# Attention with two MLPs on one core: column sums placed behind the weight conversions, and a second product that follows four steps behind the first

## The chip, the cores and the metric

One core of a Trainium2 chip. A time is the device time of one execution in microseconds (us), the median of several runs. "PE" is TensorE, "DVE" VectorE, "ACT" ScalarE, "POOL" GpSimd and "SP" SyncE, which issues the DMAs. L99 is line 99 of the kernel before.

## The reference

Batch 4, 8 heads, 576 tokens of head dimension 64, so 2304 rows of 512 for the two MLPs (512 to 2048 to 512). All of it is float32.

```python
rel = pos[:, None] - pos[None, :]
mask = (rel >= 0) & (rel < 128)
scores = np.where(mask, q @ k.T / sqrt(64) + slopes * -np.abs(rel), -1e9)
attn = softmax(scores)            # by rows
x = (attn @ v), heads side by side # 2304 x 512

r = np.maximum(x @ w_in1, 0.0)
x = (s * (r * r) + b) @ w_out1     # first MLP: s and b are scalars
h = np.maximum(x @ w_in2, 0.0)
out = (h * h) @ w_out2             # second MLP
```

## The kernel before, in words

A float32 number is kept as two parts, a rounded `hi` and the rest `lo` (`split`, L96 to L102: ACT copies, DVE subtracts), and a product is three matmuls: hi by hi, lo by hi, hi by lo. The weights arrive as 64-bit words and are converted in the kernel by `convert` (L106 to L124): ACT L119, DVE L120, ACT L121, DVE L122, one POOL addition L123, then the split (ACT L99, DVE L102 into `wil` or `wol`). A weight matrix pair is four groups of four steps (`w..0` to `w..3`).

Tokens go through the first MLP in blocks of 256: `a0` to `a7`, and `a8`, which holds the four tails of 64 tokens. The blocks `a0` to `a2` are done in two halves (`a` for steps 0 to 7, `c` for 8 to 15), because the weights of the second half are not there yet. The attention of later blocks runs as pieces between the MLP's steps (matmuls at L245, L270 and L281; the softmax's DVE instructions at L186 to L194; L268 scales probabilities before PE transposes them at L270).

The function `mlp` (L334) makes one step out of `first` (12 matmuls into a PSUM tile `h`, L357; then ACT takes the relu at L367, DVE squares at L368, and the split writes a tile `g`) and one `last` (the 12 matmuls of the second product, L394 or L403, which read `g`). A list `todo` holds the steps whose second product is outstanding. A step's `last` follows when the list is longer than `LAG = 2` (one for wide steps of 512 tokens, L384). So between a step's first product and its second stand two other steps. Tiles `g` come from a tag with three buffers. Pieces of other work come in through the list `behind`, spread over a share `span` of the steps.

Since b is a scalar, its part in the first MLP's output is b times the column sums of `w_out1`. POOL forms them in `csum`: `sum_rows` (L499) adds the hi and the lo part of each of the 16 steps, 32 additions (L502). `sum_column` (L541) adds over the partitions with four matmuls by `ones` (`pc`, L544), and DVE makes `bcol`, which ACT adds at L531 when the first MLP's result is fetched for the second (`fetch`).

After the attention its pools are closed and a pool `bp` opens, with tiles `gw` of 512 tokens (two buffers). In that stage the blocks `a7` and `a8` run as two jobs side by side, `a8` six steps behind, while the second MLP's weights are fetched and converted through three buffers `st`. Then come the second MLP's blocks `b0`, `b1`, `b2` (512 tokens), `btail` (256) and `b3`.

Every instruction is recorded in program order, and a scheduler with a model of time then sets the order on each engine. `tc.issue_after(x)` makes it place what follows behind instruction x. An engine runs its instructions in that order, so a wait holds up all that stands behind it.

Of the kernel before, what the change touches and what calls it, by code (L numbers as in the profile page):

```python
# [8 lines left out]
F32 = mybir.dt.float32  # L9
F32R = mybir.dt.float32r  # L10
# [3 lines left out]
ALU = mybir.AluOpType  # L14
PSUM = bass.MemoryType.PSUM
P = 128
# [3 lines left out]
def attention_mlp2_kernel(ctx, tc, first0, first1, qkv0, qkv1, qkvt, w_in1, w_out1, s_in, b_in, w_in2, w_out2, out):  # L20
# [7 lines left out]
    nc = tc.nc  # L28
# [9 lines left out]
    BLK = 256  # L38
# [9 lines left out]
    mp = ctx.enter_context(tc.tile_pool(name="mp", bufs=2))  # L48
# [18 lines left out]
    csum = const.tile([P, DM], F32, tag="csum", name="csum")  # L67
# [23 lines left out]
    def split(hi, lo, src, copy, sub):  # L91
        copy(hi, src)
        sub(lo, src, hi.bitcast(F32))
# [10 lines left out]

    n_g = [0]

    marks = []

    def convert(words, hi, lo):

        l32, h32 = words[..., 0], words[..., 1]
        with tc.issue_after(marks[-4]) if len(marks) > 3 else nullcontext():
            nc.scalar.activation(l32, l32.bitcast(U32), AF.Copy, scale=2.0 ** -29)  # L119
        nc.vector.scalar_tensor_tensor(l32, h32, -2 ** 31, l32, ALU.bitwise_and, ALU.bitwise_or)  # L120
        nc.scalar.activation(h32.bitcast(F32), h32.bitcast(F32), AF.Copy, scale=2.0 ** -112)  # L121
        nc.vector.tensor_scalar(h32, h32, 3, None, ALU.logical_shift_left)  # L122
        nc.gpsimd.tensor_tensor(l32, h32, l32, ALU.add)  # L123
        split(hi, lo, l32.bitcast(F32), act_copy, dve_sub)  # L124

    last_load = []
# [3 lines left out]
    def group_loads(g, wts, w_in, w_out, staging, steps):  # L130
# [22 lines left out]
        def conv(i):  # L153
            _, k, n, step = parts[i]
            if k not in wts[g]:
                for j in (k, k + 1):
                    wts[g][j] = wp.tile([P, GF, DM], F32R, tag=f"{GTAGS[j]}{g}", name=f"{GTAGS[j]}{g}")
            hi, lo = wts[g][k], wts[g][k + 1]
            part = (slice(None), slice(n, n + step)) if k else (slice(None), slice(None), slice(n * P, (n + step) * P))
            convert(places.pop(i).rearrange("p a (n w) -> p a n w", w=2), hi[part], lo[part])  # L160
# [172 lines left out]
    def mlp(jobs, wts, second, fs, behind=(), span=0.8, lead=0, n_out=2):  # L333

        pos = [[psum("o", f"o{nm}{i}") for i in range(n_out)] for nm, _, _ in jobs]  # L340
        w = n_out * P if second is second_n else BLK
        behind = list(behind)
        todo, done, left, made = [], 0, len(behind), {}
        n_steps = max(1, int(len(fs) * len(jobs) * span))

        def first(f, n):
            nm, x, _ = jobs[n]
            if n not in made:
                made[n] = x() if callable(x) else x
            xh, xl = made[n]  # L350
            g, j = divmod(f, GF)
            wih, wil = wts[g][0], wts[g][1]
            ph = psum("h", f"h{nm}_{f}")[:, :w]
            k = 0
            for cc in range(NCC):
                for w_, x_ in ((wih, xh), (wih, xl), (wil, xh)):
                    nc.tensor.matmul(ph, w_[:, cc, j * P:(j + 1) * P], x_[:, cc, :],  # L357
                                     start=(k == 0), stop=(k == 3 * NCC - 1))
                    k += 1
            n_g[0] += 1  # L360
            if w > BLK:
                gh = pools["bp"].tile([P, 2, w], F32R, tag="gw", name=f"g{nm}_{f}")
                r = pools["bp"].tile([P, w], F32, tag="rw", name=f"r{nm}_{f}", bufs=1)
            else:
                gh = mp.tile([P, 2, BLK], F32R, tag="g", name=f"g{nm}_{f}", bufs=3)
                r = mp.tile([P, BLK], F32, tag="r", name=f"r{nm}_{f}")
            nc.scalar.activation(r, ph, AF.Relu)  # L367
            nc.vector.scalar_tensor_tensor(r, ph, 0.0, r, ALU.max, ALU.mult)  # L368
            split(gh[:, 0, :], gh[:, 1, :], r, act_copy, dve_sub)
            todo.append((f, n, gh))  # L370

        def last():
            f, n, gh = todo.pop(0)
            second(pos[n], wts[f // GF], f % GF, gh, f == fs[0], f == fs[-1])
            if f == fs[-1]:
                jobs[n][2](pos[n])

        order = sorted((k + lead * n, n, f) for n in range(len(jobs)) for k, f in enumerate(fs))
        for _, n, f in order:
            while len(behind) > left * max(0, n_steps - done - 1) // n_steps:  # L380
                behind.pop(0)()
            first(f, n)
            done += 1
            if len(todo) > (1 if w > BLK else LAG):  # L384
                last()
        while todo:
            last()
# [23 lines left out]
    def finish1(nm, dram):  # L411
        def f(po):
            for t in range(2):
                xo = result(f"xo{nm}{t}")
                act_copy(xo, po[t])
                nc.sync.dma_start(dram[:, 2 * t:2 * t + 2, :].rearrange("p a n -> p (a n)"), xo)
        return f
# [17 lines left out]
    LAG = 2  # L435
    FS = list(range(NF))
    wts1, wts2 = [], []
    pools = {"ps": ps}

    def psum(tag, name):  # L440
        return pools["ps"].tile([P, DM], F32, tag=tag, name=name)
# [18 lines left out]
    def half(i, behind, span=1):  # L460
        mlp([(f"a{i}", xs[i], finish1(f"a{i}", half_dram[i]))], wts1, second_t, FS[:HF], behind, span)

    def other(i, behind, span=1):
        mlp([(f"c{i}", xs[i], finish1(f"c{i}", acc_dram[i]))], wts1, second_t, FS[HF:], behind, span)
# [33 lines left out]
    nc.sync.dma_start(b_sb, b_in.partition_broadcast(P))  # L498
    def sum_rows(g, j):  # L499

        for w in (wts1[g][2], wts1[g][3]):
            nc.gpsimd.tensor_tensor(csum, csum, w[:, j, :].bitcast(F32), ALU.add)  # L502

    nc.gpsimd.memset(csum, 0.0)
    sums = [lambda g=g, j=j: sum_rows(g, j) for g in range(NG) for j in range(GF)]
    tails = [[lambda b=b, hp=hp: tail_unit(b, hp) for hp in range(H // 2)] for b in range(B)]
    for i in range(NHALF, LAST - 1):
        more = attn(i + 2) if i + 2 < LAST and i + 2 > 4 else []
        pending += tails[i - 3] if i > 2 else []
        mlp([(f"a{i}", xt.pop(blocks[i]), finish1(f"a{i}", acc_dram[i]))], wts1, second_t, FS, zipped((pending + more[:5], 2), (sums[:4], 1)))  # L510
        pending = more[5:]
        del sums[:4]
# [4 lines left out]
    bp = pools["bp"] = ctx.enter_context(tc.tile_pool(name="bp", bufs=2))  # L517
    n_g[0] = -1

    def fetch(nm, drams, scaled=True):  # L520

        xi = bp.tile([P, NCC, BLK], F32, tag="xi", name=f"xi{nm}")
        with tc.issue_after(last_load[0]) if last_load else nullcontext():
            nc.sync.dma_start(xi, drams[0])
        if len(drams) > 1:
            for o in range(0, NCC, 2):
                xj = bp.tile([P, 2, BLK], F32, tag="xj", name=f"xj{nm}{o}", bufs=1)
                nc.sync.dma_start(xj, drams[1][:, o:o + 2, :])
                nc.vector.tensor_tensor(xi[:, o:o + 2, :], xi[:, o:o + 2, :], xj, ALU.add)
        for o in range(NCC if scaled else 0):  # L530
            nc.scalar.activation(xi[:, o, :], xi[:, o, :], AF.Identity, bias=bcol[:, o:o + 1], scale=s_sb)  # L531
        return xi
# [14 lines left out]
    def fetch_y(i):  # L547
        return fetch(f"b{i}", [acc_dram[i]] + half_dram[i:i + 1])

    def load_y(b):  # L550
# [5 lines left out]
    y0 = []  # L556
    mlp([(f"a{i}", xt.pop(blocks[i]), finish1(f"a{i}", acc_dram[i])),
         (f"a{LAST}", x_tail, finish1(f"a{LAST}", acc_dram[LAST]))], wts1, second_t, FS,
        [sum_column] + [lambda u=u: y0.append(fetch_y(u)) for u in range(2)], 0.9, 6)

    def in_bp(i, nm):
        return bp.tile([P, 1, 2 * DM], I32, tag="st", name=nm, bufs=3)
# [62 lines left out]
```

## Time and profile before

| | us |
|---|---|
| median of 3 runs (1007.28, 1007.93, 1010.74) | 1007.93 |
| the profiled execution | 1010.16 |
| its span, first to last instruction | 1008.4 |
| PE busy in it | 974.3 |
| DVE, ACT, POOL busy | 522.2, 490.2, 130.4 |

Busy time of PE is modelled with the length of a matmul in the pipeline, so a busy PE can still start its matmuls later than it could. How many matmuls start in a stretch, beside the distance of two of them where nothing waits, tells more. A row of a timeline gives the start, the length, the engine, the line and the tiles, and in brackets the idle time ahead of it and what ended that.

### The profile page before, as it was taken

The numbers are of one execution on the slowest core, as the hardware profiler recorded it, in microseconds if no ns is written. First come the engines' busy times: TensorE is split into PE (matmuls) and PEld (weight loads), VectorE is DVE, ScalarE is ACT, GpSimd is POOL, SyncE is SP. The second block draws the span as 40 slices with busy tenths as digits, with TensorE's granted clock in tenths as the row PEclk, the third lists the DMA queues.
The fourth block names the chain that finished last, engine by engine and source line by source line (L and its number), as shares of the span: only waits on it lengthen the run. The fifth ranks groups of instructions, "written<-read, shape, count | busy, mean of one in ns | idle before, by whom it ended". The sixth has DMA issues, their size and how long they took to land.

```text
span 1008.4 us, 16815 instructions
## 1 busy us (share of the span) xinstructions
PE 974.3 (97%) x6504; PEld 854.1 (85%) x6504; DVE 522.2 (52%) x1236; ACT 490.2 (49%) x1157; POOL 130.4 (13%) x118
## 2 busy tenths in 40 slices
PE   6899889999999999999999899999999999999997
PEld 4689778999989999899999888778888888898886
DVE  6997998443564444544265787754223222432222
ACT  7977766454555445554355666664222312322221
POOL 4653655000000000000010312310000000000000
PEclk9799989999999999999999999999999999999999
DMA  8135423111221211211052444422000100100001
GB/s 333 43 129 167 162 88 106 53 53 35 60 67 46 72 34 52 75 54 39 9 184 74 131 173 147 147 83 74 11 1 5 59 1 0 43 1 22 1 1 42
DMA packets 46928, 72.39 MB, mean 72 GB/s; under 512 B 6656, under 2 KB 27136, under 8 KB 46848
## 3 DMA queue, kind: packets, MB, share of 16 engines
q1 hardware_dynamic: 46848, 71.32, 21.8%
q8 instruction: 51, 0.84, 0.3%
q14 instruction: 29, 0.24, 0.1%
HBM read 59.77 MB, written 11.53 MB: 71 GB/s over the span
## 4 chain that ended last, share of the span: by engine, by line
PE 75%; DVE 9%; DMA 9%; ACT 4%; issue 2%; SPq 0%; POOL 0%; ACTq 0%; DVEq 0%; POOLq 0%
PE ob L403 15%; PE hb L357 14%; PE ha L357 13%; PE oa L394 13%; DMA st<-w_in 4%; PE oc L394 3%; PE s L245 3%; PE hc L357 3%; PE u L281 3%; DMA st<-w_out 2%; PE hbtail L357 2%; PE t L270 2%; PE obtail L403 2%; DVE wol L102 1%; DVE wil L102 1%
## 5 line engine op out<-in xcount | busy, mean ns | idle before, releaser
L394 PE MATMUL oa<-ga,woh 128*128 128x256 f32 x960 | 189.6, 289 | 7.3 <-ACT ga L99 3.9
L403 PE MATMUL ob<-woh,gb 128*128 128x512 f32 x512 | 168.9, 391 | 1.4 <-ACT gb L99 1.3
L394 PEld LDWEIGHTS oa<-ga,woh 128*128 128x128 f32 x960 | 152.2, 192 | 14.0 <-DVE ga L102 5.2
L394 PE MATMUL oa<-ga,wol 128*128 128x256 f32 x480 | 135.6, 286 | 0.1
L368 DVE SCALAR_TENSOR_TENSOR rb<-hb,rb 128x512 f32<-128x512 f32 x64 | 44.1, 690 | 147.4 <-ACT rb L367 147.2
L403 PEld LDWEIGHTS ob<-woh,gb 128*128 128x128 f32 x512 | 95.9, 188 | 23.8 <-ACT gb L99 3.3
L367 ACT ACTIVATE rb<-hb 128x512 f32<-128x512 f32 x64 | 38.2, 597 | 156.5 <-PE hb L357 152.0
L123 POOL TENSOR_TENSOR st<-st 128x512 int32<-128x512 int32 (+1 forms) x50 | 70.3, 1407 | 235.1 <-DVE st L122 177.4
L403 PE MATMUL ob<-wol,gb 128*128 128x512 f32 x256 | 99.7, 389 | 0.0
L394 PEld LDWEIGHTS oa<-ga,wol 128*128 128x128 f32 x480 | 92.2, 192 | 1.2 <-issue 0.9
L368 DVE SCALAR_TENSOR_TENSOR ra<-ha,ra 128x256 f32<-128x256 f32 x120 | 50.0, 419 | 62.9 <-ACT ra L367 62.4
L102 DVE TENSOR_TENSOR ga<-ra,ga 128x256 fp32r<-128x256 f32 x120 | 65.8, 552 | 29.0 <-ACT ga L99 28.4
L99 ACT ACTIVATE ga<-ra 128x256 fp32r<-128x256 f32 x120 | 49.5, 416 | 42.4 <-DVE ra L368 41.7
L102 DVE TENSOR_TENSOR gb<-rb,gb 128x512 fp32r<-128x512 f32 x64 | 45.5, 711 | 44.0 <-ACT gb L99 43.8
L367 ACT ACTIVATE ra<-ha 128x256 f32<-128x256 f32 x120 | 45.0, 378 | 43.6 <-PE ha L357 39.0
L99 ACT ACTIVATE gb<-rb 128x512 fp32r<-128x512 f32 x64 | 40.4, 632 | 47.7 <-DVE rb L368 35.6
L120 DVE SCALAR_TENSOR_TENSOR st<-st 128x512 int32<-128x512 int32 (+1 forms) x50 | 47.3, 950 | 26.3 <-ACT st L119 25.8
L119 ACT ACTIVATE st<-st 128x512 int32<-128x512 uint32 (+1 forms) x50 | 40.5, 814 | 35.2 <-DMA st<-w_out 19.3
L403 PEld LDWEIGHTS ob<-wol,gb 128*128 128x128 f32 x256 | 48.1, 188 | 9.7
L190 ACT ACTIVATE pr<-pr,nd 128x256 f32<-128x256 f32 (+1 forms) x96 | 45.1, 473 | 3.8 <-DVE nd L186 3.4
L121 ACT ACTIVATE st<-st 128x512 f32<-128x512 f32 (+1 forms) x50 | 40.5, 813 | 7.0 <-DVE st L120 7.0
L186 DVE CUSTOM_DVE_ANT_0 pr<-s,bases 128x256 f32<-128x256 f32 (+1 forms) x96 | 32.1, 386 | 19.4 <-PE t L270 15.0
(204 smaller groups left out, 2387.1 us busy)
## 6 DMA issues: line engine op xcount, KB each, us to landing
st<-w_out SPq DMA_DIRECT2D x20, 512.0 KB, 3.9
st<-w_in SPq DMA_DIRECT2D x8, 1024.0 KB, 6.8
st<-w_in SPq DMA_DIRECT2D x16, 512.0 KB, 4.8
st<-w_out SPq DMA_DIRECT2D x6, 1024.0 KB, 8.9
raw<-qkv SPq DMA_DIRECT2D x36, 128.0 KB, 2.6
xib<-acc SPq DMA_DIRECT2D x9, 512.0 KB, 4.4
out<-obb SPq DMA_DIRECT2D x16, 256.0 KB, 2.0
raw<-qkv SPq DMA_DIRECT2D x24, 160.0 KB, 2.9
```

The source lines that it names most:

```text
L99: return nc.scalar.activation(o, i, AF.Copy)
L102: nc.vector.tensor_tensor(o, a, b_, ALU.subtract)
L119: nc.scalar.activation(l32, l32.bitcast(U32), AF.Copy, scale=2.0 ** -29)
L120: nc.vector.scalar_tensor_tensor(l32, h32, -2 ** 31, l32, ALU.bitwise_and, ALU.bitwise_or)
L121: nc.scalar.activation(h32.bitcast(F32), h32.bitcast(F32), AF.Copy, scale=2.0 ** -112)
L123: nc.gpsimd.tensor_tensor(l32, h32, l32, ALU.add)
L190: nc.scalar.activation(pr, pr, AF.Exp, bias=nmx, scale=-1.0, accum_out=den)
L357: nc.tensor.matmul(ph, w_[:, cc, j * P:(j + 1) * P], x_[:, cc, :], start=(k == 0), stop=(k == 3 * NCC - 1))
L367: nc.scalar.activation(r, ph, AF.Relu)
L368: nc.vector.scalar_tensor_tensor(r, ph, 0.0, r, ALU.max, ALU.mult)
L394: nc.tensor.matmul(po[o // 2][:, (o % 2) * BLK:(o % 2 + 1) * BLK], w_[:, j, o * P:(o + 1) * P], g[:, gi, :], start=(start and n == 0 and o ...
L403: nc.tensor.matmul(po[t], g[:, gi, t * P:(t + 1) * P], w_[:, j, :], start=(start and n == 0), stop=(stop and n == 2))
```

## The change

It does four things.

- `sum_rows` is placed behind the last POOL addition of the first MLP's conversions (`issue_after(adds[-1])`). It is the same 32 additions.
- Once `bp` is open, steps of 256 tokens lag by four instead of two. That is the stage of `a7` and `a8`, and `btail`.
- For that, five tiles `g` live at once: of every five steps in that time, two take a tile of tag `gw` and use half of it.
- In the list of `a7` and `a8`, two empty pieces come first and the span is 0.6 instead of 0.9, so `sum_column` comes at step 7 instead of step 0, and the two fetches at steps 11 and 15 instead of 9 and 18.

```diff
@@ def convert
-        nc.gpsimd.tensor_tensor(l32, h32, l32, ALU.add)
+        adds.append(nc.gpsimd.tensor_tensor(l32, h32, l32, ALU.add).ins)
@@ def mlp, first
-                gh = mp.tile([P, 2, BLK], F32R, tag="g", name=f"g{nm}_{f}", bufs=3)
+                if "bp" in pools and n_g[0] % 5 > 2:
+                    gh = pools["bp"].tile([P, 2, 2 * BLK], F32R, tag="gw", name=f"g{nm}_{f}")[:, :, :BLK]
+                else:
+                    gh = mp.tile([P, 2, BLK], F32R, tag="g", name=f"g{nm}_{f}", bufs=3)
@@ def mlp
-            if len(todo) > (1 if w > BLK else LAG):
+            if len(todo) > (1 if w > BLK else 4 if "bp" in pools else LAG):
@@ def sum_rows
-        for w in (wts1[g][2], wts1[g][3]):
-            nc.gpsimd.tensor_tensor(csum, csum, w[:, j, :].bitcast(F32), ALU.add)
+        with tc.issue_after(adds[-1]):
+            for w in (wts1[g][2], wts1[g][3]):
+                nc.gpsimd.tensor_tensor(csum, csum, w[:, j, :].bitcast(F32), ALU.add)
@@ the call of mlp for a7 and a8
-        [sum_column] + [lambda u=u: y0.append(fetch_y(u)) for u in range(2)], 0.9, 6)
+        [lambda: None] * 2 + [sum_column] + [lambda u=u: y0.append(fetch_y(u)) for u in range(2)], 0.6, 6)
```

The order on the engines, at three places. First POOL, before: a piece of its queue while the weights of group 2 are converted (`st..` are staged weights at L123, `csum` the sums).

```order
L123 TENSOR_TENSOR st21_1102<-st21_1102 128x1024
L123 TENSOR_TENSOR st22_1225<-st22_1225 128x1024
L502 TENSOR_TENSOR csum_90<-csum_90,woh2_1475 128x512
L123 TENSOR_TENSOR st23_1258<-st23_1258 128x1024
L502 TENSOR_TENSOR csum_90<-csum_90,wol2_1476 128x512
```

And POOL in the change, at the end of the first MLP's conversions (L124 is the old L123, L507 the old L502).

```order
L124 TENSOR_TENSOR st31_1676<-st31_1676 128x1024
L124 TENSOR_TENSOR st33_1751<-st33_1751 128x512
L124 TENSOR_TENSOR st34_1815<-st34_1815 128x512
L124 TENSOR_TENSOR st35_1817<-st35_1817 128x512
L507 TENSOR_TENSOR csum_90<-csum_90,woh0_317 128x512
L507 TENSOR_TENSOR csum_90<-csum_90,wol0_318 128x512
```

All 32 additions to `csum`, which stood between the 14 conversions from `st10` to `st35`, now follow `st35` one after another.

Second DVE, before: the queue around the first squares of block `a0` (`ra0_0`, `ra0_1`), which free the PSUM tiles that PE's next step writes.

```order
L120 SCALAR_TENSOR_TENSOR st11_480<-st11_480 128x1024
L193 TENSOR_SCALAR nd0_1_2_553<-nd0_1_2_553 128x4
L194 RECIPROCAL nd0_1_2_553<-nd0_1_2_553 128x4
L368 SCALAR_TENSOR_TENSOR ra0_0_362<-ha0_0_348,ra0_0_362 128x256
L268 TENSOR_SCALAR f0_1_2woh_554<-f0_1_2woh_554,nd0_1_2_553 128x256 x2
L102 TENSOR_TENSOR wil1_340<-st10_337,wih1_339 128x4x256
L368 SCALAR_TENSOR_TENSOR ra0_1_429<-ha0_1_415,ra0_1_429 128x256
```

And the same place in the change.

```order
L121 SCALAR_TENSOR_TENSOR st11_480<-st11_480 128x1024
L194 TENSOR_SCALAR nd0_1_2_553<-nd0_1_2_553 128x4
L195 RECIPROCAL nd0_1_2_553<-nd0_1_2_553 128x4
L269 TENSOR_SCALAR f0_1_2woh_554<-f0_1_2woh_554,nd0_1_2_553 128x256 x2
L102 TENSOR_TENSOR wil1_340<-st10_337,wih1_339 128x4x256
L372 SCALAR_TENSOR_TENSOR ra0_0_362<-ha0_0_348,ra0_0_362 128x256
L372 SCALAR_TENSOR_TENSOR ra0_1_429<-ha0_1_415,ra0_1_429 128x256
```

The first square now stands behind the two scalings (old L268) and behind a weight subtraction. Such exchanges are found on PE, ACT and DVE up to the first steps of `c0` and `c1`; from there to the end of `a6` the order is the same.

Third PE, before: the second product of step 5 of block `a8` (`ga8_5`) in the stage with two jobs.

```order
L357 MATMUL ha8_6_6827<-xtailh_6224,wih1_339 128x256
L357 MATMUL ha8_6_6827<-xtaill_6225,wih1_339 128x256
L357 MATMUL ha8_6_6827<-xtailh_6224,wil1_340 128x256
L394 MATMUL oa80_6230<-ga8_5_6766,woh1_709 128x256 x2
L394 MATMUL oa80_6230<-ga8_5_6766,wol1_710 128x256
```

And the same second product in the change.

```order
L358 MATMUL ha8_7_6865<-xtailh_6224,wih1_339 128x256
L358 MATMUL ha8_7_6865<-xtaill_6225,wih1_339 128x256
L358 MATMUL ha8_7_6865<-xtailh_6224,wil1_340 128x256
L398 MATMUL oa80_6230<-ga8_5_6754,woh1_709 128x256 x2
L398 MATMUL oa80_6230<-ga8_5_6754,wol1_710 128x256
```

It followed the first product of `a8`'s step 6, and now follows that of step 7.

## Rows read from the trace of the kernel before

**Rows 1.** The page, part 1: busy us, share of the span and instructions of each engine.

```profile
PE 974.3 (97%) x6504; PEld 854.1 (85%) x6504; DVE 522.2 (52%) x1236; ACT 490.2 (49%) x1157; POOL 130.4 (13%) x118
```

**Rows 2.** Timeline of PE, 491 to 498 us (start, length): two matmuls, no waits.

```profile
495.12 0.28 PE L357 MATMUL ha<-x3h,wil 128*128 128x256 f32 x1
495.24 0.28 PE L357 MATMUL ha<-x3h,wih 128*128 128x256 f32 x1
```

**Rows 3.** Busy time by stretch; the first row names the columns.

```profile
core 0: us, PE busy (x) PEld busy (x) DVE busy (x) ACT busy (x) POOL busy (x), PEclk, DMA share, GB/s
40.00:60.00 20.00, 16.33 (x122) 13.37 (x121) 19.79 (x27) 14.72 (x32) 16.50 (x9) 0.91 0.47 174
120.00:140.00 20.00, 14.94 (x101) 12.09 (x100) 19.15 (x29) 13.07 (x28) 14.07 (x10) 0.83 0.55 177
165.00:211.00 46.00, 45.94 (x397) 42.61 (x396) 24.54 (x75) 23.41 (x65) 3.20 (x3) 1.00 0.20 59
560.00:600.00 40.00, 34.59 (x259) 32.04 (x258) 30.21 (x53) 26.80 (x58) 8.55 (x8) 1.00 0.46 152
```

**Rows 4.** Timeline of PE, 125 to 134 us: the first and last of three stalls.

```profile
130.13 0.41 PE L270 MATMUL t<-ident,pr 128*128 128x128 f32 x2 [1.65 <-DVE pr L268]
...
132.82 1.11 PE L270 MATMUL t<-ident,pr 128*128 128x128 f32 x4 [0.75 <-ACT pt L99]
```

**Rows 5.** Timeline of DVE, 120 to 136 us: the chain ahead of those stalls.

```profile
125.30 2.05 DVE L102 TENSOR_TENSOR wol<-st,woh 128x1024 fp32r<-128x1024 f32 x1 [0.17 <-ACT woh L99]
127.27 0.41 DVE L102 TENSOR_TENSOR x1l<-u,x1h 128x256 fp32r<-128x256 f32 x1
127.60 0.92 DVE L193 TENSOR_SCALAR nd<-nd 128x4 f32<-128x4 f32 x1
...
128.77 4.17 DVE L268 TENSOR_SCALAR pr<-pr,nd 128x256 f32<-128x256 f32 x4
```

**Rows 6.** Timeline of DVE, 160 to 176 us: kinds of instruction of rows 5, undisturbed.

```profile
168.56 1.13 DVE L268 TENSOR_SCALAR pr<-pr,nd 128x256 f32<-128x256 f32 x4
...
175.28 0.17 DVE L193 TENSOR_SCALAR nd<-nd 128x4 f32<-128x4 f32 x1 [0.38 <-ACT pr L190]
```

**Rows 7.** Timeline of DVE, 40 to 54 us.

```profile
40.09 1.22 DVE L102 TENSOR_TENSOR wol<-st,woh 128x1024 fp32r<-128x1024 f32 x1
...
44.50 2.48 DVE L120 SCALAR_TENSOR_TENSOR st<-st 128x1024 int32<-128x1024 int32 x1
46.90 1.23 DVE L193 TENSOR_SCALAR nd<-nd 128x4 f32<-128x4 f32 x1
...
48.57 2.42 DVE L268 TENSOR_SCALAR f_2woh<-f_2woh,nd 128x256 f32<-128x256 f32 x2
```

**Rows 8.** Groups of instructions by line, POOL: the column sums.

```profile
L502 POOL TENSOR_TENSOR csum<-csum,woh 128x512 f32<-128x512 f32 x16 | 25.2, 1573 | 8.4 <-ACT woh L99 7.8
L502 POOL TENSOR_TENSOR csum<-csum,wol 128x512 f32<-128x512 f32 x16 | 23.4, 1460 | 4.9 <-DVE wol L102 4.1
```

**Rows 9.** Groups by line and form, DVE, 165 to 215 us: one instruction per attention piece.

```profile
L193 DVE TENSOR_SCALAR nd<-nd 128x4 f32<-128x4 f32 x4 | 1.8, 442 | 1.4 <-ACT pr L190 1.4
```

**Rows 10.** Timelines of DVE and PE, 190 to 214 us: scaling, then transposes.

```profile
196.57 1.13 DVE L268 TENSOR_SCALAR pr<-pr,nd 128x256 f32<-128x256 f32 x4
...
200.04 0.38 PE L270 MATMUL t<-ident,pr 128*128 128x128 f32 x2
```

**Rows 11.** Timeline of PE, 555 to 606 us: two of its six stalls.

```profile
562.08 0.50 PE L394 MATMUL oa<-ga,woh 128*128 128x256 f32 x2 [0.93 <-ACT ga L99]
...
576.02 0.50 PE L394 MATMUL oa<-ga,woh 128*128 128x256 f32 x2 [1.54 <-ACT ga L99]
```

**Rows 12.** Timeline of ACT, 555 to 600 us, ahead of the first of them.

```profile
561.05 0.68 ACT L119 ACTIVATE st<-st 128x512 int32<-128x512 uint32 x1 [0.95 <-DMA st<-w_out]
561.63 0.40 ACT L99 ACTIVATE ga<-ra 128x256 fp32r<-128x256 f32 x1
```

**Rows 13.** Timeline of PE, 498 to 606 us: the sum column.

```profile
503.70 1.05 PE L544 MATMUL pc<-ones,csum 128*128 128x1 f32 x8 [0.75 <-ACT xoa L99]
```

More of the change, by code (lines that the diff above doesn't have):

```diff
@@ L105, in attention_mlp2_kernel @@
     n_g = [0]
+    adds = []
     marks = []
```

## The prediction

> **What bounds the kernel now.** I read the page's busy times first, then the granted clock and PE's busy share by stretches, then PE's stalls one by one, and last what the engine that PE waited for was doing. PE is the bound: it is busy for 974.3 of 1008.4 us, DVE for half the span and POOL for an eighth [rows 1]. So a change can gain only where PE waits, where its clock is down, or where its matmuls start later than they could. Where nothing waits, two matmuls of 256 columns start 0.12 us apart [rows 2]; a step of 24 takes 2.88 us. Three stretches stand out [rows 3]. From 40 to 60 us PE is idle for 3.67 us, and the granted clock averages 0.91. From 120 to 140 us it is idle for 5.06 us with the clock at 0.83: a third of that time, 6.8 us, at 1.2 GHz instead of 2.4, which is 3.4 us of work. In both DVE is busy for over 19 of 20 us and POOL for 14 to 16. From 560 to 600 us PE starts 259 matmuls, worth 31.1 us at 0.12, with a clock of 1.00; a few are wide ones, so some 8 us are lost there, 5.41 of them as idle time. From 165 to 211 us PE is idle for 0.06 us, with a clock of 1.00.
>
> **The column sums.** What holds PE up at 130 us is read from DVE. PE's transposes wait for the scaling at L268 [rows 4]. Four scalings take 4.17 us there [rows 5] and 1.13 us where no addition of POOL runs beside them [rows 6]; the small instruction at L193 takes 0.92 against 0.17; the weight subtraction takes 2.05 against 1.22 [rows 7]. That is 3.04 + 0.75 + 0.83 = 4.6 us on one chain without a gap, while POOL adds column sums back to back. An instruction that reads PSUM at the same time (`x1l`) takes its usual 0.41 us [rows 5]. So it is the sums, 25.2 + 23.4 = 48.6 us on POOL [rows 8], that hold DVE's SBUF work, and the order shows that all 32 leave this stretch. Of the 4.6 us I take 3.8, since the last stall of the three ends with ACT and not with DVE [rows 4]; of the 3.4 us of clock I take 2.7, since PE idles before the sums too. Sum: **6.5 us gained** at 120 to 140 us. Bounds: 2 (only the first stall of 1.65 us goes, and something else is late next) and 8 (all of the chain and of the clock).
>
> From 40 to 60 us the same three kinds of instruction are long: 2.48 at L120, 1.23 at L193, 2.42 for two scalings [rows 7], some 4.1 us above their usual lengths (1.2 as the subtraction of the same size, 0.17 and 0.6). But in the new order the square that frees PE's PSUM tile stands behind the two scalings (0.6) and a weight subtraction (1.2), where it stood ahead of them; and conversions, which stay, hold DVE as the sums do. I take **0**, with bounds of 4.1 gained and 1.8 lost. The exchanges of order up to 100 us, where DVE is as full, I count into these bounds.
>
> **Where the sums go.** They run in one block after the last conversion, at about 161 us, and their 48.6 us reach to about 210 or later. The stretch from 165 to 211 us has DVE busy for 24.5 of 46 us and PE without idle time [rows 3], so there is room, but the attention goes on: four pieces with one L193 each [rows 9] and four scalings. By rows 5 and 6 a piece's chain grows by up to 0.75 + 3.04 = 3.8 us. In the undisturbed trace the scalings end at 197.70 and the transposes start at 200.04 [rows 10], 2.3 us later. What is left is 1.5 us of stall a piece; for the three pieces that lie well inside the block, **4.5 us lost**. Bounds: 0 (the room takes it all) and 18.6 (four pieces at 3.8, and one fall of the clock as at 131 us, 3.4). I take the value nearer to the lower end because the slack is seen in a row, and DVE is half free.
>
> Here a rule of the notes speaks against the change. The Trainium skill, page "SBUF — State Buffer", section "Who interferes with whom", says that VectorE and GpSimd share one pair of ports, that the one that starts first keeps it for its whole instruction, and that the other is blocked. The trace agrees on which instructions are held: the scaling is, the one with a PSUM input is not. By the rule alone the same 32 additions hold the port as long after the move as before it; the sum would then be the next term by itself, 6 us gained, and the case is the second rival.
>
> **Lag of four.** The six stalls from 560 to 600 us are of one kind: a second product waits for `g` from ACT or DVE, 0.39 to 1.54 us [rows 11]. ACT copied that `g` late, since it had stood on a conversion whose DMA was late by 0.95 us [rows 12]. These are waits for something late, not for something slow: ACT works 26.8 and DVE 30.2 of the 40 us [rows 3]. Two more steps of distance are 2 x 2.88 = 5.76 us, more than any of the stalls. But if the stretch shrinks from 40 to 32 us, the same 30.2 us of DVE would fill it to 94 per cent, so not all comes back. **6 us gained**; bounds 2 and 8. The price of the lag, second products that free the weights' tiles and PSUM later, lies inside the stage: a tile of weights comes free two steps later on that account, and the stage's waits, which now fall away, are as long. In `btail` PE has no wait to lose, and the borrowed tiles are idle then: 0.
>
> **The sum column** costs the same matmuls at step 7 as at step 0. Its wait of 0.75 us [rows 13] ended with ACT's copy out of PSUM, for a tile that the next product `ha7_0` now writes first; the wait passes to that product. 0, with a bound of 0.75 gained.
>
> **Sum.** -6.5 + 0 + 4.5 - 6 + 0 = -8.0 us. The profiled execution took 1010.16 us, of which the span is 1008.4; it would take 1002.2. It lies 2.2 us above the median of the runs shown, 1007.93, so against the median the forecast is **999.9 us, say 1000**.
>
> **The rivals.**
>
> The block stalls PE (slower). All four pieces behind 161 us pay the full 3.8 us, and the clock falls once: 18.6 us instead of 4.5. For it: the same chain at 125 to 133 us cost about that much, for one piece. Against it: DVE is half free, and slack is seen. The sum is then +6.1, 1014 us. It decides against the change from 12.5 us of cost on, beyond which the two gains are spent, and shows as slower from 15.5. Chance 0.09.
>
> The move is worth nothing. The sums hold DVE as long in the block as they did before, and PE waits there for the 6.5 us that it gains at 130 us: each of the four pieces costs 1.6 us instead of the 1.5 of three. The sum is then the lag's -6, and the time 1001.9 us. For it: the additions are the same 32, and their 48.6 us are longer than the 46 in which PE has no wait. Against it: DVE is busy for over 19 of 20 us where they stand now, and for half the time where they will. Chance 0.12.
>
> The lag only shifts the wait. ACT and DVE work at their rate, not late, and what PE wins before 600 us it waits for in `b0`, whose steps lag by one as before. Then the lag gives 2, and the sum is -4: 1004 us. For it: the 94 per cent. Against it: the conversions are not bound to this stretch. Chance 0.20.
>
> The block hides. DVE's free half takes it, and both gains come whole: -8 - 8 = -16, 992 us. For it: PE idles nowhere from 165 to 211 us. Against it: transposes follow scalings by 2.3 us only. Chance 0.20.
>
> The change does not do what it says: new stalls of the exchanged order before 100 us take back what the sums give, and the lag gives the 2 us: about 1007. Chance 0.06.
>
> **How the numbers follow.** My forecast has the other 0.33. Its own range, with the bounds of its terms, is 994 to 1006. For 8 in 10 the range reaches to the hiding block and to the shifted wait, and leaves out the slower rival and the lowest end: **990 to 1009**. About 0.3 per cent, 3.0 us, can be told from no change, so faster means under 1004.9. The forecast lies there nearly whole (0.31), the worthless move mostly (0.11), of the shifted wait two thirds (0.13), and the hiding block (0.20): 0.75. Slower is the first rival with a little of the rest, 0.10. The same is what remains, 0.15.
>
> **What would show it.** Right: from 120 to 140 us no addition at the old L502, four scalings in about 1.2 us, PE idle under 2 us and a clock near 1.00; from 161 us on 32 additions in a row, scalings of up to 4 us, and a few PE waits on L268; from 560 to 600 us no PE wait over 0.3 us and the stage some 6 us shorter; `ha7_0` ahead of `pc` with the wait of about 0.7 us. Wrong: PE idle for over 8 us between 160 and 220 us, or a loss in `b0` as large as the gain before it, or stalls between 60 and 100 us, where there are none now.

## The result, and the profile after

| | before | change |
|---|---|---|
| median, us | 1009.18 (7 runs, 1007.28 to 1010.74) | 1015.3 (7 runs, 1012.57 to 1020.97) |
| the profiled execution, us | 1010.16 | 1018.52 |
| its span, us | 1008.4 | 1016.7 |

The change is slower: the ratio is 1.0065, with a 95% interval of 1.0041 to 1.0090. The forecast was 1000 us with a range of 990 to 1009.

PE does the same work; the same engine is the bound as in [rows 1]. The page, part 1, of the changed kernel:

```profile
PE 978.9 (96%) x6504; PEld 858.5 (84%) x6504; DVE 526.6 (52%) x1236; ACT 489.5 (48%) x1157; POOL 125.4 (12%) x118
```

Busy time by stretch in the changed kernel (columns as in [rows 3]), with one more stretch, that of `b0`:

```profile
core 0: us, PE busy (x) PEld busy (x) DVE busy (x) ACT busy (x) POOL busy (x), PEclk, DMA share, GB/s
40.00:60.00 20.00, 19.70 (x143) 16.55 (x143) 15.91 (x31) 16.00 (x34) 3.98 (x3) 0.81 0.46 174
120.00:140.00 20.00, 16.15 (x105) 13.66 (x104) 14.91 (x30) 15.30 (x31) 3.10 (x2) 0.74 0.51 166
165.00:211.00 46.00, 39.45 (x309) 36.72 (x310) 36.61 (x61) 18.00 (x49) 39.40 (x29) 0.93 0.15 44
560.00:600.00 40.00, 39.98 (x332) 39.66 (x331) 31.01 (x55) 28.94 (x61) 9.82 (x9) 1.00 0.52 173
600.00:680.00 80.00, 72.59 (x326) 56.94 (x326) 59.30 (x88) 51.69 (x92) 18.98 (x19) 1.00 0.40 128
```

And that stretch in the kernel before:

```profile
600.00:680.00 80.00, 78.64 (x367) 64.11 (x366) 55.05 (x88) 53.17 (x94) 20.17 (x18) 1.00 0.40 125
```

Against [rows 3]: at 40 to 60 us PE is idle for 0.30 us instead of 3.67, but the clock is 0.81 instead of 0.91. At 120 to 140 us it is idle for 3.85 instead of 5.06, with a clock of 0.74 instead of 0.83. From 165 to 211 us it is idle for 6.55 instead of 0.06, and the clock has fallen to 0.93: this is the block. From 560 to 600 us it is idle for 0.02 instead of 5.41. From 600 to 680 us it is idle for 7.41 instead of 1.36.

Idle time leaves out a slow clock, so I also use the **loss**: for each matmul of a trace, how much later the next one starts than is usual (the median) after a matmul of that shape in that trace, summed over a stretch. It counts waits and slow clock alike. In us:

| loss, us | 0-40 | 40-160 | 160-200 | 200-560 | 560-600 | 600-680 | all |
|---|---|---|---|---|---|---|---|
| before | 21.9 | 19.9 | 2.0 | 10.9 | 8.4 | 3.1 | 66.0 |
| change | 22.0 | 17.6 | 11.5 | 12.0 | 1.0 | 10.6 | 74.7 |

So the 8.3 us between the spans are +9.6 at the block, -2.3 ahead of it, -7.4 from 560 to 600 us, +7.5 in `b0`, and 1 us of small change between.

**The block.** Timeline of the changed kernel, 163 to 188 us, POOL, DVE and PE:

```profile
163.64 1.24 DVE L194 TENSOR_SCALAR nd<-nd 128x4 f32<-128x4 f32 x1
...
166.42 5.44 DVE L269 TENSOR_SCALAR pr<-pr,nd 128x256 f32<-128x256 f32 x4
...
167.74 1.28 POOL L507 TENSOR_TENSOR csum<-csum,wol 128x512 f32<-128x512 f32 x1
...
169.09 1.27 POOL L507 TENSOR_TENSOR csum<-csum,woh 128x512 f32<-128x512 f32 x1
...
172.64 0.85 PE L246 MATMUL s<-qk 64*128 64x256 f32 x10 [2.75 <-DVE qk L102]
...
181.47 5.30 DVE L269 TENSOR_SCALAR pr<-pr,nd 128x256 f32<-128x256 f32 x4
...
187.15 0.39 PE L358 MATMUL hc<-x0h,wih 128*128 128x256 f32 x1 [2.45 <-DVE rc L372]
```

Four scalings (old L268) take 5.44 and 5.30 us, against 1.13 undisturbed [rows 6] and 4.17 in the kernel before [rows 5]: each waits for about one whole addition of 1.27 or 1.28 us. But PE's longest waits, 2.75 and 2.45 us, end with the split of `qk` and with a square, DVE instructions that stand behind the scalings in its queue. That a DVE instruction which runs in a mode with two ports, as `tensor_scalar` can, or which has two inputs in SBUF, is held for a whole POOL instruction is what the Trainium skill says on the page "SBUF — State Buffer", section "Who interferes with whom"; the trace agrees for the scaling (5.44 / 4 = 1.36 us each, and the additions start 1.34 to 1.45 us apart there).

**Ahead of it.** Timeline of the changed kernel, 120 to 130 us, ACT, DVE and PE:

```profile
120.80 0.74 ACT L99 ACTIVATE qk<-raw 128x640 fp32r<-128x640 f32 x1 [3.63 <-DMA raw<-qkv]
...
125.82 0.54 PE L358 MATMUL ha<-x1h,wih 128*128 128x256 f32 x2 [1.02 <-ACT x1h L96]
...
126.70 1.14 DVE L269 TENSOR_SCALAR pr<-pr,nd 128x256 f32<-128x256 f32 x4
...
128.39 0.69 ACT L120 ACTIVATE st<-st 128x512 int32<-128x512 uint32 x1 [0.82 <-DMA st<-w_out]
...
129.89 1.12 PE L271 MATMUL t<-ident,pr 128*128 128x128 f32 x4 [1.54 <-ACT pt L99]
```

The scalings take 1.14 us, as predicted. They could start little earlier, for ACT stood for 3.63 us waiting for a load of `raw`, from which `qk` and all that follows are made. It did so in the kernel before, in a row of ACT that I had not read:

```profile
122.02 0.74 ACT L99 ACTIVATE qk<-raw 128x640 fp32r<-128x640 f32 x1 [3.06 <-DMA raw<-qkv]
```

From ACT's `qk` to the end of the scalings it is now 7.0 us instead of 10.9, so the chain did become shorter. But behind the scalings the next wait, 1.54 us, ends with ACT, which took `pt` late because it had stood on a conversion whose load was late by 0.82 us. The clock fell sooner and for longer. Busy time by 5 us, the changed kernel:

```profile
125.00:130.00 5.00, 2.64 (x11) 2.08 (x12) 4.07 (x11) 4.18 (x12) 0.00 (x0) 0.61 0.98 303
130.00:135.00 5.00, 5.00 (x26) 4.34 (x27) 3.98 (x6) 3.67 (x7) 2.88 (x2) 0.50 0.18 68
135.00:140.00 5.00, 5.00 (x38) 4.70 (x38) 3.52 (x5) 3.25 (x6) 0.22 (x1) 0.86 0.01 3
```

The kernel before:

```profile
125.00:130.00 5.00, 2.53 (x20) 1.92 (x18) 4.76 (x8) 4.17 (x13) 4.76 (x4) 1.00 0.86 253
130.00:135.00 5.00, 3.28 (x17) 2.01 (x17) 5.00 (x7) 2.16 (x3) 2.45 (x2) 0.64 0.44 161
135.00:140.00 5.00, 5.00 (x31) 4.87 (x32) 4.94 (x7) 3.76 (x9) 2.02 (x2) 0.68 0.00 0
```

**`b0`.** Timeline of the changed kernel, 622 to 655 us, ACT and PE:

```profile
622.32 0.66 ACT L120 ACTIVATE st<-st 128x512 int32<-128x512 uint32 x1 [2.59 <-DMA st<-w_in]
...
623.44 0.60 ACT L371 ACTIVATE rb<-hb 128x512 f32<-128x512 f32 x1
...
626.17 0.61 ACT L99 ACTIVATE gb<-rb 128x512 fp32r<-128x512 f32 x1
...
626.84 0.50 PE L407 MATMUL ob<-woh,gb 128*128 128x512 f32 x1 [1.46 <-ACT gb L99]
...
654.00 0.50 PE L407 MATMUL ob<-woh,gb 128*128 128x512 f32 x1 [1.62 <-ACT gb L99]
```

PE waits for `g`. ACT makes it late: it stood for 2.59 us on a conversion whose load was not there, and the relu of a step whose matmuls had long ended came behind it. It is the pattern of [rows 11] and [rows 12], one stage later. Of the 32 POOL additions of these conversions 17 start after `b0`'s first matmul, against 18 in the kernel before: PE reaches `b0` with less waiting, but hardly more of the conversions is done by then.

**The sum column.** Its wait went where it was expected, to `ha7_0`, with the same 0.75 us as in [rows 13]:

```profile
512.16 0.38 PE L358 MATMUL ha<-x3h,wih 128*128 128x256 f32 x1 [0.75 <-ACT xoa L99]
```

### The profile page after: what moved, and what is told of

It is laid out like the page before. It is cut to its first block, busy times and chain, and to the rows that moved or that the text cites. A ratio compares the mean times of both kernels' runs of the same rounds, so it can differ in the third digit from the quotient of the medians.

```text
span 1016.7 us, 16817 instructions
## 1 busy us (share of the span) xinstructions
PE 978.9 (96%) x6504; PEld 858.5 (84%) x6504; DVE 526.6 (52%) x1236; ACT 489.5 (48%) x1157; POOL 125.4 (12%) x118
## 4 chain that ended last, share of the span: by engine, by line
PE 75%; DMA 9%; DVE 8%; ACT 6%; issue 2%; SPq 0%; ACTq 0%; DVEq 0%
PE ob L407 15%; PE hb L358 14%; PE ha L358 13%; PE oa L398 12%; DMA st<-w_out 6%; PE s L246 4%; PE u L282 3%; PE oc L398 3%; PE hc L358 3%; PE hbtail L358 2%; PE obtail L407 2%; PE t L271 2%; DMA st<-w_in 2%; ACT st L120 1%; DVE st L121 1%
## 5 line engine op out<-in xcount | busy, mean ns | idle before, releaser
L398 PE MATMUL oa<-ga,woh 128*128 128x256 f32 x960 | 187.5, 288 | 1.9 <-DVE ga L102 1.8
L124 POOL TENSOR_TENSOR st<-st 128x512 int32<-128x512 int32 (+1 forms) x50 | 68.5, 1371 | 284.3 <-DVE st L123 223.0
L102 DVE TENSOR_TENSOR ga<-ra,ga 128x256 fp32r<-128x256 f32 x120 | 56.4, 473 | 32.5 <-ACT ga L99 31.4
```

Source lines behind the costliest of these rows:

```text
L102: nc.vector.tensor_tensor(o, a, b_, ALU.subtract)
L124: adds.append(nc.gpsimd.tensor_tensor(l32, h32, l32, ALU.add).ins)
L398: nc.tensor.matmul(po[o // 2][:, (o % 2) * BLK:(o % 2 + 1) * BLK], w_[:, j, o * P:(o + 1) * P], g[:, gi, :], start=(start and n == 0 and o ...
```

## The experiments

Each is compared with runs of the kernel before on the same chip. "1.005 [1.003, 1.007]" is the ratio to it with its interval. The losses of all of them (us, of the profiled execution):

| run | median us | ratio | 40-160 | 160-200 | 200-560 | 560-600 | 600-680 |
|---|---|---|---|---|---|---|---|
| sums moved alone | 1015.0 | 1.0050 [1.0032, 1.0067] | 17.4 | 11.5 | 11.1 | 5.1 | 4.8 |
| lag and list alone | 1009.6 | 1.0008 [0.9998, 1.0018] | 19.8 | 2.2 | 10.9 | 1.5 | 9.1 |
| change, sums in quarters | 1006.0 | 0.9961 [0.9946, 0.9977] | 16.6 | 1.0 | 10.8 | 1.6 | 10.4 |
| s and b folded into g | 1011.5 | 1.0026 [1.0014, 1.0038] | 27.9 | 2.2 | 22.0 | 5.6 | 9.5 |
| before, half the conversions | 1006.0 | 0.9970 [0.9955, 0.9984] | 19.4 | 2.3 | 10.8 | 8.1 | -0.1 |
| lag and list, half the conversions | 1000.7 | 0.9915 [0.9888, 0.9942] | 21.1 | 2.1 | 10.9 | 1.3 | -0.1 |
| moved, quarters, old lag | 1014.2 | 1.0057 [1.0037, 1.0078] | 17.3 | 11.3 | 13.3 | 4.3 | 5.1 |
| quarters in place | 1018.1 | 1.0087 [1.0063, 1.0111] | 35.5 | 4.8 | 22.4 | 5.2 | 4.4 |
| sums spaced | 1006.1 | 0.9968 [0.9956, 0.9981] | 16.9 | 0.9 | 14.0 | 6.3 | 3.8 |
| spaced, lag and list | 1006.1 | 0.9975 [0.9965, 0.9984] | 15.5 | 0.5 | 12.1 | 1.4 | 10.0 |
| lag and list, four buffers | 1009.5 | 1.0001 [0.9992, 1.0011] | 20.5 | 2.0 | 10.9 | 6.0 | 2.8 |
| spaced, four buffers | 1006.2 | 0.9966 [0.9954, 0.9979] | 16.6 | 0.4 | 14.3 | 5.9 | 4.7 |
| spaced, lag and list, four buffers | 1005.2 | 0.9959 [0.9947, 0.9972] | 16.2 | 0.4 | 11.6 | 5.5 | 5.6 |
| moved, no sums | 1004.5 | 0.9959 [0.9947, 0.9971] | 17.4 | 0.8 | 11.6 | 6.3 | 3.8 |
| moved, halves | 1004.2 | 0.9955 [0.9940, 0.9969] | 16.0 | 2.5 | 12.3 | 5.6 | 3.0 |
| moved, halves, conversions in halves | 1001.9 | 0.9928 [0.9909, 0.9947] | 14.9 | 1.5 | 11.4 | 4.0 | 4.1 |

**1. The parts alone.** The sums moved, without the rest (the first and the fourth piece of the diff), and the rest without them.

> Only the first part of the change: the 32 additions behind the last conversion; lag, list and tiles as before. My theory (the block makes PE wait, 160 to 200 us, for 9.6 us more than before; between 36 and 160 us only some 2 us come back): about 7 us slower than before, 1016 us, ratio 1.007, with the same PE waits between 160 and 190 us as in the changed kernel. Rival (the moved sums are neutral and the loss sits in the stage of a7 and a8 and in b0): 1007 to 1009 us, ratio under 1.001.

> Only the other parts: lag of four, places of wide tiles, the new list; the sums stay where they were before. My theory (the lag only shifts the wait: what PE wins from 560 to 600 us it waits for in b0): within 2 us of before, 1007 to 1010 us, with no PE wait from 560 to 600 us and 6 to 8 us more lost in b0. Rival (b0 lost only because the late block had disturbed the stage): 6 us faster, 1003 us, ratio 0.994.

Busy time by stretch with the sums moved alone, 160 to 200 us:

```profile
160.00:180.00 20.00, 14.46 (x106) 12.74 (x106) 19.29 (x32) 9.94 (x32) 18.98 (x15) 0.91 0.27 80
180.00:200.00 20.00, 17.40 (x140) 16.42 (x140) 12.45 (x17) 5.99 (x15) 18.90 (x15) 0.91 0.14 46
```

The first is slower by the whole of the change, and PE stands idle there for 8.1 us with a clock of 0.91, as in the changed kernel (8.0 us). The second is no different from before, since it gains 6.9 us from 560 to 600 us and loses 6.0 more in `b0`. Both theories hold, and the parts add up: 1.0050 and 1.0008 against 1.0065 for the whole.

**2. One addition cut into four.** In the changed kernel:

```diff
             for w in (wts1[g][2], wts1[g][3]):
-                nc.gpsimd.tensor_tensor(csum, csum, w[:, j, :].bitcast(F32), ALU.add)
+                for c in range(0, DM, P):
+                    nc.gpsimd.tensor_tensor(csum[:, c:c + P], csum[:, c:c + P], w[:, j, c:c + P].bitcast(F32), ALU.add)
```

> The changed kernel, but each addition of 512 columns done as four of 128 in the same place; the order on all other engines is the same. My theory (each DVE instruction on SBUF waits for the one addition that is under way, so the length of one counts): the scalings of the block take under 3 us for four instead of 5.4, the loss from 160 to 200 us falls from 11.5 us to under 6, and the time to about 1009 us, 6 us under the changed kernel. Rival (the additions hold DVE for their sum, however cut): no gain, 1015 us or more, as POOL's fixed cost makes the block longer.

Busy time by stretch, 160 to 200 us, with quarters:

```profile
160.00:180.00 20.00, 19.55 (x164) 17.90 (x163) 15.48 (x38) 11.62 (x35) 20.00 (x40) 1.00 0.34 98
180.00:200.00 20.00, 20.00 (x174) 18.83 (x173) 9.97 (x27) 9.68 (x26) 20.00 (x45) 1.00 0.14 47
```

And two rows of DVE's timeline there:

```profile
163.53 1.97 DVE L269 TENSOR_SCALAR pr<-pr,nd 128x256 f32<-128x256 f32 x4
...
172.05 2.07 DVE L269 TENSOR_SCALAR pr<-pr,nd 128x256 f32<-128x256 f32 x4
```

POOL is busy without a break, longer than with whole additions, and PE loses 1.0 us instead of 11.5. Four scalings take 2.0 us. So here it isn't the time that POOL is busy that counts, but how long one of its instructions keeps DVE; run 3 has a case where quarters do not help. This version is faster than both kernels.

**3. The same with the old lag, and quarters in place.** The order on PE, ACT and DVE of the first is that of the sums moved alone, instruction by instruction.

> Sums moved behind the conversions and cut into quarters of 128 columns; lag, list and tiles as before. The order on all engines but POOL is that of the run with the sums moved alone (1015.0 us). My theory (the length of one addition counts): the waits from 160 to 200 us go, 1005 us, 10 us less than that run; and as the lag is worth nothing, within 2 us of the 1006.0 us with lag. Rival (the lag helps where the block does not disturb): 1009 us or more.

> The kernel before with each column sum cut into quarters, placed where the scheduler wants them, which is between 36 and 170 us as before, in a somewhat other order. My theory (length counts, place does not): the sums hold DVE for 0.5 us at a time instead of 1.3 to 1.6, and 2 to 4 us come back between 36 and 140 us: 1005 to 1006 us. Rival (the place counts too, since DVE is full there): 1008 us or more.

Both expectations failed. Timeline of the first, 187 to 203 us:

```profile
187.68 14.58 DVE L102 TENSOR_TENSOR gc<-rc,gc 128x256 fp32r<-128x256 f32 x1 [0.71 <-ACT gc L99]
...
195.70 1.68 POOL L505 TENSOR_TENSOR csum<-csum,wol 128x128 f32<-128x128 f32 x4
...
197.34 1.68 POOL L505 TENSOR_TENSOR csum<-csum,woh 128x128 f32<-128x128 f32 x4
...
202.31 0.58 PE L395 MATMUL oc<-gc,woh 128*128 128x256 f32 x1 [10.09 <-DVE gc L102]
```

One subtraction of 256 columns took 14.58 us, while some 35 additions of 0.41 us ran past it on POOL, and PE stood for 10.09 us. With quarters in place no wait is that long, but a small instruction of DVE takes 4.40 us, the time of some ten additions (0.41 us from one to the next there):

```profile
86.04 4.40 DVE L193 TENSOR_SCALAR nd<-nd 128x4 f32<-128x4 f32 x1 [1.69 <-ACT pr L190]
```

So with short additions a DVE instruction can wait for many. In run 2 it did not, with the same order on every engine up to 499 us; what decides is not settled. It is no accident of one execution: the seven times with the old lag lie between 1013.6 and 1017.8 us, the six of run 2 between 1003.5 and 1006.5. Quarters in place also came in another order, so its 35.5 us of loss from 40 to 160 us are not the waits alone.

**4. Halves, and no sums.** Both with the order of the sums moved alone on PE, ACT and DVE; the second shows what the block costs and the order does not.

> The sums moved alone, each addition cut into two of 256 columns, back to back; the same order elsewhere. If a DVE instruction waits for one addition whatever its length, 160 to 200 us loses 3 to 6 us, 1007 to 1010 us, and no DVE instruction there takes over 2 us. If additions without a pause can pass a waiting DVE instruction again and again, as in the one case of 14.6 us with quarters, a DVE instruction of several us shows here too and the time is 1012 us or more.

> The 32 additions are left out (the column sums stay zero, so the second term of the first MLP's output is missing); everything else is the kernel with the sums moved alone, with the same order on PE, ACT and DVE. My theory (the block as a whole costs what that run loses from 160 to 200 us over this one): 160 to 200 us loses about 1 us instead of 11.5, the time is 1005 us, 10 us under the 1015.0 us with the block, and the spaced sums at 1006.1 us cost under 1.5 us. Rival (the new order itself costs the time, not the additions): over 1010 us.

Busy time by stretch with halves, 160 to 200 us:

```profile
160.00:180.00 20.00, 18.21 (x151) 16.30 (x150) 18.75 (x36) 8.94 (x27) 20.00 (x26) 1.00 0.26 73
180.00:200.00 20.00, 20.00 (x174) 18.89 (x173) 12.34 (x28) 9.94 (x26) 20.00 (x27) 1.00 0.14 48
```

And four scalings on DVE:

```profile
173.98 2.80 DVE L269 TENSOR_SCALAR pr<-pr,nd 128x256 f32<-128x256 f32 x4
```

The block costs 1015.0 - 1004.5 = 10.5 us as whole additions and nothing that shows in the time as halves (1004.2 us; from 160 to 200 us they lose 2.5 us, where 0.8 is lost without sums), though four scalings still take 2.80 us instead of 1.13: PE's chain has that much room, and not 5.4. No DVE instruction in that stretch took over 1.5 us. Without any sums the stretch that the prediction was about is still no better:

```profile
120.00:140.00 20.00, 15.72 (x103) 13.21 (x104) 15.78 (x32) 14.23 (x30) 3.76 (x3) 0.74 0.43 150
```

From 120 to 140 us the clock is 0.74 and PE idle for 4.28 us, with no addition of column sums on POOL at all. So the sums alone did not set the time there. That they cost something where they stood is likely (1008.5 against 1004.5 us), but the order differs too, and no run has the old order without them. The loss of one profile also varies by a microsecond or so. Ten kernels of the two tables share the new order up to 160 us and have no sums before 157: they lose 15.5 to 17.6 us from 40 to 160 us, and 6.3 to 8.3 of these from 120 to 140. Five have the old order with whole sums in place: they lose 19.4 to 21.1, and 7.4 to 9.8. So some 3 us come back ahead of the block, but only about 1 of them where 6.5 were forecast.

**5. Sums one at a time.** Each addition follows a POOL copy of one column of the newest `g`, so they spread over `a3` to `a6`.

```diff
+        t = nc.gpsimd.tensor_copy(tick, last_g[0][:, 0, :1].bitcast(F32))
+        with tc.issue_after(t.ins):
+            nc.gpsimd.tensor_tensor(csum, csum, wts1[g][k][:, j, :].bitcast(F32), ALU.add)
```

> The sums later still and one at a time: each of the 32 additions follows a tiny POOL copy that reads the newest g, so that they spread over the blocks a3 to a6, eight in a block. The order on PE, ACT and DVE up to the start of a6 is that of the changed kernel; lag, list and tiles as before. My theory (an addition holds up at most one DVE instruction, by at most 1.3 us, and the chain has room for one): PE loses nothing new from 160 to 500 us, the 2 us from before 160 us stay, 1004 to 1006 us. Rival (any addition beside the attention costs PE time): 1008 us or more.

> Spaced sums with the change's lag, places and list, three buffers of staged weights. My theory (the lag is worth nothing, with or without the block): within 1.5 us of the 1006.1 us of spaced sums with the old lag. Rival (the lag is worth 2 us or more once nothing else disturbs): 1004 us or less.

The first holds in its time, 1006.1 us, but not in "nothing new": 14.0 us are lost from 200 to 560 us where it is 11.6 without sums, so spacing is not quite free. The second holds too: with and without lag and list the median is 1006.1 us.

**6. What gives the lag's gain back.** The last two groups of the second MLP's weights are left out and the first two used in their place:

```diff
-for g in range(NG)]
+for g in range(2)]
...
-    pieces = sum(pieces[1:], [])
+    pieces = pieces[1][:1] + [lambda: wts2.extend(wts2[:2])] + pieces[1][1:] + [lambda: None] * 31
```

> The kernel before, but the last two groups of the second MLP's weights are neither loaded nor converted: b0 and all later blocks use the first two groups in their place. This leaves out 16 of 32 conversions, those that lie beside b0. My theory (b0's small waits come from conversions ahead of g on ACT that stand waiting for their load): b0 loses under 1 us instead of 3.1, the stage before it is unchanged with some 8 us lost from 560 to 600 us, and the time is 2 to 3 us shorter, 1006 us.

> Lag of four, wide places and the new list as in the run with these alone, and the last two groups of the second MLP's weights left out as in the other run. My theory (the lag's gain is lost in b0 to the conversions): b0 loses under 1 us instead of 9, the gain from 560 to 600 us stays, and the time is 1000 to 1002 us, 5 us less than the kernel before without those conversions. Rival (the lag itself hurts b0, by tiles or PSUM that come free later): b0 still loses 5 us or more, and both kernels without conversions take the same time.

Busy time from 600 to 680 us, the kernel before without those conversions, and then with lag and list:

```profile
600.00:680.00 80.00, 80.00 (x382) 67.36 (x381) 26.12 (x40) 25.83 (x46) 1.86 (x2) 1.00 0.06 20
```

```profile
600.00:680.00 80.00, 80.00 (x361) 66.47 (x360) 22.88 (x34) 23.77 (x42) 0.00 (x0) 1.00 0.06 20
```

Both come out as expected, 1006.0 and 1000.7 us. With no conversions beside it `b0` loses nothing, and the lag is worth 5.3 us. So the lag itself does no harm; the conversions that are still to be done when PE comes sooner take the gain. Whether it is their loads or their work on ACT and DVE, these two runs do not tell, since both are left out.

**7. Four buffers for the staged weights.** If the loads are what the conversions wait for, a fourth buffer should help.

> Lag of four, wide places and the new list, sums as before, but four buffers for the second MLP's staged weights instead of three (room from sharing a tag for xj and from the sums' tile, whose column is formed before the attention's pools close). My theory (b0 waits for conversions that stand on ACT waiting for a load, and the load waits for one of three buffers): b0 loses under 5 us instead of 9, 1003 to 1005 us. Rival (ACT and DVE are simply full): 1009 us as with three.

> Spaced sums, lag of four with its places and list, and four buffers for staged weights. If both theories hold the gains add up: 2 to 3 us from the sums and 4 to 6 from the lag that is no longer given back, 999 to 1002 us. If spaced sums cost PE time it is 1004 us, if four buffers do nothing 1006 us.

> Spaced sums and four buffers, but lag and list as before. My theory (loads come earlier, so g stands behind waiting conversions less often, here in the stage of a7 and a8 too): 1001 to 1004 us, and what the lag itself is worth with four buffers is its difference to the run with it, 1 to 3 us. Rival (only the lag brings anything in that stage): 1005 us.

None of the three came in its time. In the first `b0` does lose under 5 us (2.8), but 6.0 are now lost from 560 to 600 us, and the time is 1009.5. Busy time of that run, 580 to 640 us:

```profile
580.00:600.00 20.00, 17.25 (x125) 16.37 (x123) 18.60 (x32) 16.21 (x34) 6.16 (x7) 0.91 0.61 190
600.00:620.00 20.00, 18.90 (x94) 16.07 (x94) 17.95 (x28) 14.75 (x26) 7.05 (x6) 1.00 0.71 231
620.00:640.00 20.00, 18.73 (x79) 14.07 (x77) 18.87 (x28) 16.66 (x30) 9.79 (x7) 1.00 0.57 185
```

The conversions end some 20 us earlier, and DVE is now busy for 18 to 19 of 20 us, where it was 14 to 16 with three buffers. From 560 to 680 us ACT waits 11.8 us for loads of weights instead of 15.8, and 8.8 us are lost instead of 10.6. That a full DVE has taken the place of the waits for loads is likely, but not shown. With spaced sums (the other two) the fourth buffer brings 1 us at most by the medians (1.6 by the ratios), and the lag, four buffers or three, 1 us or nothing.

**8. The sums formed elsewhere.** s and b put in where `g` is split, so that no sums are needed.

> No column sums at all: s and b are put in where g is formed (the square times s, and b added in the two instructions of the split), so that the first MLP's output needs neither; lag and list as before but for the sum column. The instruction counts on ACT and DVE per step are the same, and fetch loses its scaling on ACT. My theory (the sums cost PE time by holding DVE between 36 and 140 us, but other things are late next): 3 to 6 us faster, 1003 to 1006 us, ratio 0.995. Rival (the sums cost nothing where they stood, since loads set the pace there): within 1 us of before.

Neither expectation holds, and the run does not tell what it was meant to. The loads of s and b, put first in the queue, delayed the first matmul from 3.97 to 6.99 us, and the two instructions of the split became longer, 507 and 484 ns against 415 and 424 in the kernel before (groups by line, 200 to 500 us):

```profile
L372 ACT ACTIVATE ga<-ra,b_sb 128x256 fp32r<-128x256 f32 x64 | 32.4, 507 | 22.2 <-DVE ra L371 21.9
L373 DVE SCALAR_TENSOR_TENSOR ga<-ra,b_sb,ga 128x256 fp32r<-128x256 f32 x64 | 30.9, 484 | 25.5 <-ACT ga L372 24.1 <-PE u L283 0.6 <-PE u_t L327 0.6
```

That lengthens every step: 22.0 us are lost from 200 to 560 us instead of 10.9.

**9. The finding carried to the conversions.** The POOL addition in `convert` cut into two as well, on top of halves for the sums.

> The kernel with the sums moved and cut into halves (1004.2 us), and the POOL additions of the weights' conversion cut into two as well; the order on the engines changes somewhat from the fourth conversion on. If the length of one POOL addition is what holds DVE in the first 140 us too, one to three us come back: 1001 to 1003 us. If loads and the conversion's own chain set the pace there, the extra instructions only lengthen it: 1004 to 1007 us.

1001.9 us, 7 us less than the kernel before and 13 less than the change: the fastest of those that leave nothing out. It is as expected, but the order differs from that of halves alone (on ACT from 40 us on, on PE from 114), so its 2.3 us are not shown to come from the length of the additions.

## Why the prediction was wrong

- **"6.5 us gained" from 120 to 140 us: failed.** The loss there went from 8.8 to 8.3 us. The three instructions became short as predicted, but I took what the chain loses as what PE gains, and priced it from its middle. Its head is ACT's wait of 3.06 us for a load, which stays; with a shorter chain the next waits end with ACT, so PE's idle time fell by 1.2 us only (5.06 to 3.85), and the clock, which was to give 2.7 us back, fell for longer (0.83 to 0.74). With no sums at all the loss there is still 8.3 us in one profile, and over all profiles about 1 us comes back (experiment 4). How much the exchanged order took of the gain is open.
- **40 to 60 us, "0" with a gain of up to 4.1:** 2.5 us less loss (6.3 to 3.8), of which 0.9 came back by 80 us. Inside the bounds.
- **The block, "4.5 us lost": mis-sized.** It lost 9.6. The direction was right. What failed is "1.5 us of stall a piece". I took 3.8 us for a piece's chain, and it grew by (1.24 - 0.17) + (5.44 - 1.13) = 5.4 us. Two pieces, not three, lie well inside the block; the third starts its scalings at 205.7 us, where the additions end. And I counted the scalings and their 2.3 us of room alone: DVE's queue is one, and the splits of `qk` and `g` and the squares behind them were late as well; PE's two longest waits, 2.75 and 2.45 us, end with such instructions. The clock, at 0.93 from 165 to 211 us, took up to 0.07 x 46 = 3.2 us of the 9.6; the 4.5 had nothing for it. This is the first rival's mechanism, at half of its 18.6 us.
- **The lag, "6 us gained": the gain came (7.4), and was given back whole.** What failed is "the conversions are not bound to this stretch", with which I held the third rival off; the sum had no term for `b0`. The conversions stand on ACT and DVE among the instructions that make `g`, and 17 of 32 were left for `b0`. This is the third rival, with 0 instead of the 2 that I left it. Experiment 6 shows that it is the conversions; whether their loads or their work sets the pace is open.
- **The sum column, 0: right.** The wait of 0.75 us went to `ha7_0`.
- **The second rival** wanted 6.5 us gained ahead and as much lost in the block; it was 2.3 and 9.6. Its ground, that the same additions hold DVE as long however they lie, is refuted by halves: they keep POOL busier in the same place (40.0 of the 40 us from 160 to 200, against 37.9 with the sums moved whole), and the time is that without sums.

Each of the two slower mechanisms stood among the rivals, but as cases that exclude each other. They lie in different stages and came together; the sum of the first rival at its measured 9.6, of nothing from the lag, and of 2.3 gained ahead is +7.3, against 6.1 between the medians. Of the signs of being wrong that the prediction names, the loss in `b0` as large as the gain before it came, and PE's idle time from 160 to 220 us reached the 8 us.

## What to carry to other kernels

Where two engines hold each other up, look at the length of one instruction before the share of busy time: moving POOL's additions whole to a half-empty stretch added 10 us, and cutting them in two took these away. Shorter still is not safe: in quarters the same additions once cost as much as whole. Before pricing a wait by the slow instructions ahead of it, follow the chain back to where it starts, and read the engine that is next in line. And a gain in one stage counts only if the work beside it, here weight conversions on the queues that also make `g`, keeps up; else the next stage waits for it.

## What was not expected of the hardware

A DVE subtraction of 128x256 took 14.58 us, while additions of 0.41 us followed one another on POOL, and another small one 4.40 us. With 64 halves (0.81 and 0.84 us in the mean of their two groups) and 32 whole additions (1.40 and 1.35 us) back to back, nothing like it was seen: from 160 to 200 us no DVE instruction took over 1.4 and 1.9 us. Why short additions can pass DVE again and again in one run and not in another with the same order stays open. The Trainium skill, on the page cited above, says that whoever issues first gets the shared pair of ports for its whole instruction; where the subtraction took 14.58 us, 35 additions that started after it went ahead of it, and there the measurement decides. What gave back 2 us ahead of the block stays open too: the order changed there as well as the place of the sums.
